# Identity products in TensorE's waits: linear attention and an FNet block with an MLP, on one Trainium2 core

## The chip, the cores and the metric

The kernel runs on 1 core of one Trainium2 chip. The metric is the device time of one execution in microseconds (us). Before the change the median of five runs is 843.5 us (841.67, 842.81, 843.5, 844.53 and 843.78). Where a stretch of one execution is described, the times are those of one further execution that was recorded with the hardware profiler.

## The reference

Four sequences (batches) of 768 rows with 8 heads of 64 columns go through causal linear attention with a decay `lam` per head. Its result `x` (768 rows of 512 columns for each batch) goes through a two-dimensional Fourier transform whose real part is added to it, a normalization of each row, and an MLP of 512 to 2048 to 512 with a ReLU. Everything is float32; the two weight matrices arrive as float64.

```
intra = einsum(q, k) * Dmask            # Dmask = lam ** (i - j), i >= j
out   = einsum(intra, v) + einsum(q * lam_pow, kv_state)
u     = x + real(fft(fft(x, axis=1), axis=2))
un    = (u - mean) / sqrt(var + 1e-6)
y     = u + relu(un @ w_ch1) @ w_ch2
```

## The kernel before, in words

**Attention** (`attn`, lines 241 to 387) cuts the 768 rows of a batch into six chunks of 128. For each chunk `attn_in` loads k, q and v (SP's queue), transposes k and q on TensorE by a product with the identity (L268, L273) and lets ScalarE copy the results out of PSUM (L270, L275); VectorE also writes the decayed copy `qs` (L279). `attn_out` multiplies k by q into scores (L292); VectorE multiplies each half of the scores by the decay (L296, tiles `sc`); TensorE updates the running state (L307, then L309 or L312 on VectorE), multiplies the old state by `qs` (L320) and the scores by v (L324). ScalarE copies the result `oT` out (L327), and `back` transposes it into rows (L340, then L342 and L343 on ScalarE). Batch 0 is "turned": the rows in mirrored order that the Fourier transform needs are made by TensorE too (`mirrored`, on tile `ds`); the other batches write their rows to DRAM and gather them mirrored (L421, L424, L429 on GpSimd's queue).

**The Fourier transform** (`fft_ln`) folds the rows by symmetry on VectorE (L410 to L413, L448 to L459), multiplies by cosine and sine tables along the rows (L483, copied out to `ys` by ScalarE at L487) and then along the columns (`width`, L496 to L501). ScalarE copies a part into `bs` (L559, L560, L562) and VectorE finishes `u` (L563 to L567).

**The normalization** (`norm`) takes statistics on VectorE (L513, L514), the root on GpSimd (L517, L518), and writes `un` on VectorE (L531; one buffer). For the first four pairs of tiles, the list `PLAIN`, TensorE transposes `un` (L536) and ScalarE copies it out to `ut` (L537), which the MLP reads. `PLAIN[0]` is the first pair of batch 0 whose rows are ready.

**The MLP** multiplies by the first weights (L600) and the second (L614) for `PLAIN`, and later, for all other rows, by a two-by-two scheme with seven products (L687, L734). The **weights** come in 32 pieces as float64 (L209, tile `raw`, four buffers shared with the MLP's hidden rows) and are turned into float32 by two ScalarE and five VectorE instructions each (L214, L216; L215, L218, L220, L221, L222). The pieces 0 to 7 fill the half of the first matrix that the first MLP half reads, 8 to 15 the half of the second matrix.

**The order of the work.** The program is written as generators that are woven together by planned durations (`weave`, `beside`, `run`): attention of batch 0 beside weight pieces; then attention of batch 1 beside the transform of batch 0 and more weight pieces; then the first half of the MLP beside what is left, and so on. On top of it a scheduler orders each engine's instructions by its own estimate of when their inputs are ready; the order in the built program is therefore not the order of the text. PSUM has five banks for the attention and the transform (`pa`) and three for the MLP (`pm`). An instruction wrapped in `keep_in_program_order` may not be placed ahead of the instruction that the text has before it on the same engine.

Of the kernel before, what the change touches and what calls it, by code (L numbers as in the profile page):

```python
# [76 lines left out]
def kernel(  # L77
# [10 lines left out]
    nc = tc.nc  # L88
# [50 lines left out]
    def new(pool, shape, tag, **kw):  # L139
        cnt[0] += 1  # L140
        return pool.tile(shape, F32, tag=tag, name=f"{tag}{cnt[0]}", **kw)

    def psum_a(shape):
        return new(pa, shape, "pa")

    def psum_m(shape):
        return new(pm, shape, "pm")

# [2 lines left out]
    ident = const.tile([128, 128], F32, name="ident")  # L154
# [128 lines left out]
    def attn_out(b, c, head):  # L283
        kT, qT, qs, kd, vt = ins.pop((b, c))
        last = c == NC - 1


        mm = nc.tensor.matmul
        pss = [psum_a([C, HP, C]) for _ in range(2)]
        for hp in range(HP):  # L290
            for hi in range(2):
                mm(pss[hi][:, hp, :], lhsT=kT[HD[hi], hp, :], rhs=qT[HD[hi], hp, :], start=True, stop=True)  # L292
        sc = []
        for hi in range(2):
            t = new(at, [C, HP, C], "sc", bufs=3)
            nc.vector.tensor_tensor(t, pss[hi], decay[:, hi::2, :], op=ALU.mult)  # L296
            sc.append(t)
        yield 1.5


        s_old, s_new = st[(c + 1) % 2], st[c % 2]
        if not last:
            pu = psum_a([128, HP, D])
            for hp in range(HP):
                for hi in range(2):
                    h = 2 * hp + hi
                    mm(pu[HD[hi], hp, :], lhsT=kd[:, h, :], rhs=vt[:, h, :], start=True, stop=True)  # L307
            if c == 0:
                nc.vector.tensor_copy(s_new, pu)  # L309
            else:  # L310
                nc.gpsimd.tensor_tensor(s_new, s_old, spow.broadcast_to([128, HP, D]), op=ALU.mult)
                nc.vector.tensor_tensor(s_new, s_new, pu, op=ALU.add)  # L312
            yield 0.9


        po = psum_a([128, HP, C])
        if c > 0:
            for hp in range(HP):
                for hi in range(2):
                    mm(po[HD[hi], hp, :], lhsT=s_old[HD[hi], hp, :], rhs=qs[HD[hi], hp, :],  # L320
                       start=(hp == 0), stop=False, skip_group_check=True)
        for hp in range(HP):
            for hi in range(2):
                mm(po[HD[hi], hp, :], lhsT=vt[:, 2 * hp + hi, :], rhs=sc[hi][:, hp, :],  # L324
                   start=(c == 0 and hp == 0), stop=(hp == HP - 1), skip_group_check=True)
        oT = new(at, [128, HP, C], "oT")
        nc.scalar.copy(oT, po)  # L327
        if b in TURNED:

            if c == 0:  # L330
                nc.scalar.copy(first, po[:, :, 0:1])
            elif c > 1:
                nc.scalar.copy(oTs[b][:, :, 0:1], po[:, :, 0:1])
        yield 2.0
        yield from head

        def back(oT, x, n=128):
            px = psum_a([C, HP, 128])
            for hp in range(HP):
                nc.tensor.transpose(px[:, hp, :], oT[:, hp, :], ident)  # L340
            px = px.rearrange("p h e -> p (h e)")
            nc.scalar.copy(x[0:n, 0:HM], px[0:n, 0:HM])  # L342
            nc.scalar.copy(x[0:n, HM:DM], px[0:n, DM - 1:HM - 1:-1])  # L343

        if b not in TURNED:
            x = xn_[b, c] = new(xp, [C, DM], "x") if c < HC else new(xn, [C, DM], "xn")
            back(oT, x)
            if c == 0:
                xd[b] = (dram.tile([S - 256, DM], F32, name=f"xa{b}"), dram.tile([257, DM], F32, name=f"xb{b}"))
                nc.scalar.dma_start(xd[b][1][256:257], x[0:1])  # L350
            elif not last:
                nc.scalar.dma_start(xd[b][0][(c - 1) * C:c * C], x)
            if c >= NC - 2:
                nc.scalar.dma_start(xd[b][1][(c - NC + 2) * C:(c - NC + 3) * C], x)
            if c == NC - 2:
                mirror_a(b)
            elif last:
                mirror_b(b)
            yield 1.7
            return  # L360


        if c == 2:
            eo[b] = new_eo()

        def mirrored(m):
            if m < HC:
                back(oTs[b], eo[b][HC - 1 - m][1][:, 1, 0:DM], BLK[HC - 1 - m])
            else:
                u = xs[b, HC + NC - 1 - m] = new(xp, [128, DM], "x")  # L370
                back(oTs[b], u)

        if c > 1:
            mirrored(c - 1)
            yield 1.4
        if c > 0:
            oTs[b] = new(fp, [128, DM + 4], "ds")[:, 0:DM].rearrange("p (h c) -> p h c", h=HP)
            nc.scalar.copy(oTs[b][:, :, C - 1:0:-1], po[:, :, 1:C])
        if not last:
            x = xn_[b, c] = new(xp, [C, DM], "x") if c < HC else new(xn, [C, DM], "xn")  # L380
            back(oT, x)
            yield 1.7
        else:
            nc.scalar.copy(oTs[b][:, :, 0:1], first)
            mirrored(c)
            for t in range(HC):
                xs[b, t] = xn_.pop((b, t))
            yield 1.4
# [26 lines left out]
    def mirror_a(b):  # L415

        xa = xd[b][0]

        eo[b] = new_eo()
        for a, n in enumerate(BLK):  # L420
            gather(out=eo[b][a][1][0:n, 1, 0:DM], out_offset=None, in_=xa[:, :], in_offset=row_of(a, n))  # L421
        for t in range(2, HC):
            u = xs[b, HC + t] = new(xp, [128, DM], "x")
            gather(out=u[:, :], out_offset=None, in_=xa[:, :], in_offset=row_of(2 + t))  # L424
# [45 lines left out]
    def fft_ln(b):  # L470
# [7 lines left out]
        for i in range(5):  # L478
            ps = psum_a([128, 2, NK])
            m = 128 if i < 4 else 1  # L480
            for n in range(2):
                for a, rows in enumerate(BLK):
                    mm = nc.tensor.matmul(ps[0:m, n, :], lhsT=piece(a, i, n), rhs=cs[0:rows, a, i in (2, 3), n, :],  # L483
                                          start=(a == 0), stop=(a == 1))
# [24 lines left out]
        def norm(g):  # L509
            mv = new(np_, [128, G, 2], "mv")  # L510
            for i in range(G):
                stt = new(np_, [128, 6], "stt")
                nc.vector.bn_stats(stt, xs[b, TT[g][i]])  # L513
                nc.vector.bn_aggr(mv[:, i, :], stt)  # L514
            ve = new(np_, [128, G], "ve")
            rs = new(np_, [128, G], "rs")
            nc.gpsimd.tensor_scalar(ve, mv[:, :, 1], EPS, None, op0=ALU.add)  # L517
            nc.gpsimd.tensor_tensor(rs, ve, mhalf, op=ALU.pow)  # L518

            yield 5.0 if (b, g) == PLAIN[0] else 1.0  # L520
            plain = (b, g) in PLAIN
            if plain:
                ut = uts[b, g] = new(up, [128, KO, G * 128], "ut")
            else:

                to = utd[b, g] = dram.tile([128, KO, G * 128], F32, name=f"utd{b}{g}")
            for i in range(G):
                un = new(np_, [128, DM], "un", bufs=1)
                u = xs[b, TT[g][i]]
                for o, x in ((un[:, 0:HM], u[:, 0:HM]), (un[:, HM:DM], u[:, DM - 1:HM - 1:-1])):  # L530
                    nc.vector.tensor_scalar(o, x, mv[:, i, 0:1], rs[:, i:i + 1],  # L531
                                            op0=ALU.subtract, op1=ALU.mult)
                if plain:
                    pt = psum_a([128, KO, 128])
                    for c in range(KO):
                        nc.tensor.transpose(pt[:, c, :], un[:, 128 * c:128 * c + 128], ident)  # L536
                    nc.scalar.copy(ut[:, :, 128 * i:128 * i + 128], pt)  # L537
                else:

                    uq = new(ep, [128, DM], "e")  # L540
                    nc.vector.transpose(uq, un)
                    for r in range(0, 128, 32):
                        dst = to[:, :, 128 * i + r:128 * i + r + 32].rearrange("(a d) c n -> d c a n", d=32)
                        src = uq[r:r + 32].rearrange("p (c a n) -> p c a n", c=KO, n=32)
                        nc.sync.dma_start(dst, src)
                yield 0.7
            if plain:
                return
            for T in TT[g]:
                ud[b, T] = dram.tile([128, DM], F32, name=f"ud{b}{T}")  # L550
                nc.sync.dma_start(ud[b, T], xs.pop((b, T)))

        for t in (1, 2, 0):
            ps = psum_a([128, DM])
# [14 lines left out]
            if t == 0:  # L569
                ps = psum_a([128, DM])  # L570
# [12 lines left out]
    PLAIN, LATE = ORDER[:4], ORDER[4:]  # L583
# [289 lines left out]
```

## Time and profile before

| what | value |
|---|---|
| median of five runs | 843.5 us |
| profiled execution, own time | 841.55 us |
| its span, first to last instruction | 839.5 us |
| around the span | 2.05 us |
| mean granted TensorE clock | 0.992 |
| PE busy | 801.8 us, 96%, 4608 instructions |
| VectorE (DVE) busy | 444.9 us, 53%, 1030 instructions |
| ScalarE (ACT) busy | 181.8 us, 22%, 436 instructions |
| GpSimd (POOL) busy | 77.7 us, 9%, 102 instructions |

PE is TensorE's products, PEld its weight loads. A float32 product that isn't a transpose stands in the trace as two instructions (x2 for one product), a transpose as one. In the page's second part each digit is the busy share of one of 40 equal slices of 21 us. The clock row is the TensorE clock that was granted, in tenths of full speed. "Idle before <- X" says how long an engine stood still ahead of an instruction and what released it.

### The profile page before, as it was taken

What the parts mean: (1) busy time and instruction counts of PE and PEld (TensorE: products, weight loads), DVE (VectorE), ACT (ScalarE), POOL (GpSimd) and SP (SyncE); (2) the same over time, 40 slices, a digit from 0 to 9 for tenths busy, and PEclk for the clock granted to TensorE, in tenths of its full rate; (3) what the DMA queues carried; (4) which work ended last, traced back from release to release, by engine and by line L of the source; (5) the groups of instructions that cost most, each with busy time, mean ns of one, the idle gap of its engine ahead of it and who ended that gap; (6) DMA issues with size and microseconds to landing.
All of it is one profiled execution on the core that took longest, in us unless ns stands there. A gap on an engine that the chain in (4) does not pass through costs nothing.

```text
span 839.5 us, 11685 instructions
## 1 busy us (share of the span) xinstructions
PE 801.8 (96%) x4608; PEld 639.3 (76%) x4608; DVE 444.9 (53%) x1030; ACT 181.8 (22%) x436; POOL 77.7 (9%) x102
## 2 busy tenths in 40 slices
PE   5977799999999999999999999999999999999998
PEld 4766576767766666767847888888888888888886
DVE  6969989875822483245795551155412552145411
ACT  3762542323511111221101210022000220012100
POOL 2211121010111020121000000000000000000000
PEclk9998899999999999999999999999999999999999
DMA  9967443138832136441334011100111000110010
GB/s 241 259 155 197 120 139 131 62 84 214 201 95 70 37 75 138 101 135 38 97 72 144 0 52 43 52 7 0 51 51 51 0 1 16 51 36 1 1 38 25
DMA packets 126683, 68.87 MB, mean 82 GB/s; under 512 B 111150, under 2 KB 112174, under 8 KB 126630
## 3 DMA queue, kind: packets, MB, share of 16 engines
q1 hardware_dynamic: 121632, 55.67, 26.0%
q0 software_dynamic: 2112, 6.69, 2.4%
q10 hardware_dynamic: 2886, 5.77, 1.9%
q8 instruction: 36, 0.59, 0.3%
q14 instruction: 17, 0.14, 0.1%
HBM read 48.72 MB, written 19.40 MB: 81 GB/s over the span
## 4 chain that ended last, share of the span: by engine, by line
PE 79%; DVE 11%; issue 4%; DMA 3%; ACT 2%; POOL 1%; SPq 0%; POOLq 0%; DVEq 0%; ACTq 0%
PE p L734 23%; PE p L687 23%; PE pm L614 9%; PE pm L600 7%; PE pa L324 3%; PE pa L292 3%; PE pa L483 3%; PE pa L320 2%; PE pa L340 1%; DMA x<-xb,ix 1%; PE pa L268 1%; PE pa L307 1%; DVE stt L513 1%; DVE sc L296 1%; DMA xb<-xn 1%
## 5 line engine op out<-in xcount | busy, mean ns | idle before, releaser
L600 PE MATMUL pm<-ut,w 128*128 128x256 f32 x512 | 119.8, 383 | 0.2 <-DVE hr L606 0.2
L614 PE MATMUL pm<-w,hr 128*128 128x512 f32 x256 | 116.1, 598 | 1.3 <-DVE hr L606 1.3
L600 PEld LDWEIGHTS pm<-ut,w 128*128 128x128 f32 x512 | 94.1, 190 | 15.6 <-issue 3.4
L687 PE MATMUL p<-ur,w 128*128 128x256 f32 x384 | 93.8, 379 | 0.0
L614 PEld LDWEIGHTS pm<-w,hr 128*128 128x128 f32 x256 | 46.6, 190 | 51.4 <-issue 48.6
L687 PEld LDWEIGHTS p<-ur,w 128*128 128x128 f32 x384 | 73.0, 190 | 10.3 <-issue 0.5
L687 PE MATMUL p<-us,w1s 128*128 128x256 f32 x256 | 65.7, 379 | 0.0
L734 PE MATMUL p<-w,hs 128*128 128x256 f32 x256 | 58.0, 379 | 0.5 <-DVE y L755 0.5
L734 PE MATMUL p<-w,ha 128*128 128x256 f32 x256 | 57.9, 379 | 0.0
L734 PE MATMUL p<-w2s,hs 128*128 128x256 f32 x256 | 57.9, 379 | 0.0
L734 PEld LDWEIGHTS p<-w,hs 128*128 128x128 f32 x256 | 48.5, 190 | 7.5 <-DVE y L755 0.9
L734 PEld LDWEIGHTS p<-w2s,hs 128*128 128x128 f32 x256 | 48.6, 190 | 6.6
L687 PEld LDWEIGHTS p<-us,w1s 128*128 128x128 f32 x256 | 48.6, 190 | 6.6
L734 PEld LDWEIGHTS p<-w,ha 128*128 128x128 f32 x256 | 48.6, 190 | 6.6
L589 POOL DMA_INDIRECT out_dram<-y,ix x12 | 11.8, 987 | 408.2 <-DVE y L760 344.1
L714 ACT COPY ha<-p 128x256 f32<-128x256 f32 x32 | 11.9, 372 | 169.2 <-PE p L687 139.4
L292 PEld LDWEIGHTS pa<-qT,kT 64*128 64x128 f32 x384 | 28.2, 198 | 17.1 <-ACT qT L275 9.7
L292 PE MATMUL pa<-qT,kT 64*128 64x128 f32 x384 | 33.2, 299 | 7.1 <-ACT qT L275 6.7
L296 DVE TENSOR_TENSOR sc<-pa,decay 128x512 f32<-128x512 f32 x48 | 31.6, 683 | 12.7 <-PE pa L292 12.5
L324 PE MATMUL pa<-sc,v 128*64 128x128 f32 x384 | 31.7, 287 | 6.1 <-DVE sc L296 6.1
L725 DVE TENSOR_TENSOR ha<-p,ha 128x256 f32<-128x256 f32 x32 | 13.6, 425 | 44.8 <-ACT ha L724 44.8
L324 PEld LDWEIGHTS pa<-sc,v 128*64 128x64 f32 x384 | 23.2, 140 | 14.8 <-DVE sc L296 9.1
(144 smaller groups left out, 1139.6 us busy)
## 6 DMA issues: line engine op xcount, KB each, us to landing
raw<-in_moe_w_ch_dram SPq DMA_DIRECT2D x32, 512.0 KB, 4.9
k<-in_k_dram SPq DMA_DIRECT2D x24, 256.0 KB, 4.7
q<-in_q_dram SPq DMA_DIRECT2D x24, 256.0 KB, 5.0
v<-in_v_dram SPq DMA_DIRECT2D x24, 256.0 KB, 3.3
ud<-x SPq DMA_DIRECT2D x16, 256.0 KB, 2.3
utd<-e SPq DMA_DIRECT2D x64, 64.0 KB, 2.2
u<-ud SPq DMA_DIRECT2D x16, 256.0 KB, 2.7
ur<-utd SPq DMA_DIRECT2D x6, 512.0 KB, 4.3
```

Source lines behind the costliest of these rows:

```text
L292: mm(pss[hi][:, hp, :], lhsT=kT[HD[hi], hp, :], rhs=qT[HD[hi], hp, :], start=True, stop=True)
L296: nc.vector.tensor_tensor(t, pss[hi], decay[:, hi::2, :], op=ALU.mult)
L320: mm(po[HD[hi], hp, :], lhsT=s_old[HD[hi], hp, :], rhs=qs[HD[hi], hp, :], start=(hp == 0), stop=False, skip_group_check=True)
L324: mm(po[HD[hi], hp, :], lhsT=vt[:, 2 * hp + hi, :], rhs=sc[hi][:, hp, :], start=(c == 0 and hp == 0), stop=(hp == HP - 1), skip_group_chec ...
L483: mm = nc.tensor.matmul(ps[0:m, n, :], lhsT=piece(a, i, n), rhs=cs[0:rows, a, i in (2, 3), n, :], start=(a == 0), stop=(a == 1))
L589: nc.gpsimd.indirect_dma_start(out=out.rearrange("b s d -> (b s) d"), out_offset=row_of(2 + HC * (b + 1) + T - HC), in_=y[:, :], in_offset ...
L600: nc.tensor.matmul(ps, lhsT=w1[:, c, 128 * fc:128 * fc + 128], rhs=ut[:, c, :], start=(c == 0), stop=(c == KO - 1))
L614: nc.tensor.matmul(ps, lhsT=hr[(fc - f0) // 4][:, fc % 4, 128 * i:128 * i + 128], rhs=w2[:, fc, :], start=(fc == f0), stop=(fc == f1 - 1))
L687: nc.tensor.matmul(ps, lhsT=s2.A[a][:, kt, 128 * i:128 * i + 128], rhs=U[b][:, kt, :], start=(first and kt == 0), stop=(kt == 1), skip_gro ...
L714: nc.scalar.copy(a11, two(X))
L725: V.tensor_tensor(a22, two(Z), a22, op=ADD)
L734: nc.tensor.matmul(ps, lhsT=h[a][:, s, i, :], rhs=s2.B[b][:, i, :], start=(first and i == 0), stop=(i == HF - 1), skip_group_check=True)
```

## The change

A helper `warm(n)` takes one PSUM tile of the MLP's pool and issues `n` products of the 128x128 identity with itself into it. Nothing reads the tile. It is called in four places: after the score products of chunks 0 to 2 of batch 1 (four products each), in the last chunk of batch 0 ahead of the first and the second of its two mirrored transposes (four and six), and ahead of the first normalized rows of `PLAIN[0]` (sixteen): 38 products in all. Each is kept behind the TensorE instruction that stands before it in the text. No other line changes.

```
+    def warm(n):
+
+        ps = psum_m([128, 128])
+        for _ in range(n):
+            tc.keep_in_program_order(nc.tensor.matmul(ps, lhsT=ident, rhs=ident, start=True, stop=True))
...
                 mm(pss[hi][:, hp, :], lhsT=kT[HD[hi], hp, :], rhs=qT[HD[hi], hp, :], start=True, stop=True)
+        if b == 1 and c < 3:
+            warm(4)
         sc = []
...
         if c > 1:
+            if last:
+                warm(4)
             mirrored(c - 1)
...
             nc.scalar.copy(oTs[b][:, :, 0:1], first)
+            warm(6)
             mirrored(c)
...
             for i in range(G):
+                if (b, g, i) == (*PLAIN[0], 0):
+                    warm(16)
                 un = new(np_, [128, DM], "un", bufs=1)
```

## The prediction, made before the changed kernel had run

> **What bounds the kernel now.** I read the page first: busy shares by slice, the granted clock and the chain that ended last.
>
> ```profile
> span 839.5 us, 11685 instructions
> PE   5977799999999999999999999999999999999998
> DVE  6969989875822483245795551155412552145411
> PEclk9998899999999999999999999999999999999999
> PE 79%; DVE 11%; issue 4%; DMA 3%; ACT 2%; POOL 1%; SPq 0%; POOLq 0%; DVEq 0%; ACTq 0%
> ```
>
> From the sixth slice on (105 us) PE is the bound and nearly full. Before that it waits, VectorE is at 9 in slices 4 to 6, and two slices have a lower clock. What is won or lost before about 116 us shifts everything behind it by as much. So I read that stretch in steps of 4 us (PE, PEld, DVE, ACT and POOL busy with counts, clock, DMA).
>
> ```profile
> core 0: us, PE busy (x) PEld busy (x) DVE busy (x) ACT busy (x) POOL busy (x), PEclk, DMA share, GB/s
> 64.00:68.00 4.00, 1.70 (x10) 0.85 (x8) 4.00 (x8) 1.17 (x2) 0.46 (x1) 1.00 0.85 298
> 68.00:72.00 4.00, 3.12 (x24) 2.39 (x26) 3.89 (x9) 1.25 (x4) 0.94 (x1) 0.62 0.30 67
> 72.00:76.00 4.00, 4.00 (x46) 3.49 (x42) 2.66 (x5) 1.18 (x3) 1.11 (x1) 0.53 1.17 304
> 96.00:100.00 4.00, 1.16 (x16) 0.97 (x16) 4.00 (x8) 1.39 (x4) 0.00 (x0) 0.96 0.76 188
> 100.00:104.00 4.00, 2.05 (x20) 1.62 (x20) 3.42 (x11) 1.41 (x3) 0.95 (x2) 0.50 0.01 2
> 104.00:108.00 4.00, 4.00 (x41) 3.27 (x38) 3.93 (x8) 1.08 (x3) 1.51 (x1) 0.69 0.02 4
> ```
>
> Twice a 4 us step with little PE work (1.70, 1.16 busy) is followed by some 7 us at half clock, and VectorE is full on both occasions: PE is waiting for VectorE. The timelines of PE and of VectorE show the instructions.
>
> ```profile
> 50.49 0.66 PE L340 MATMUL pa<-ident,ds 128*128 128x128 f32 x4 [0.74 <-ACT ds L333]
> 52.46 0.66 PE L340 MATMUL pa<-ident,ds 128*128 128x128 f32 x4 [1.32 <-ACT ds L384]
> 57.78 0.43 PE L324 MATMUL pa<-sc,v 128*64 128x128 f32 x2 [1.17 <-DVE sc L296]
> 77.56 1.09 PE L324 MATMUL pa<-sc,v 128*64 128x128 f32 x14 [1.12 <-DVE sc L296]
> 93.34 0.39 PE L499 MATMUL pa<-dt,ys 128*128 128x128 f32 x2
> 93.57 0.39 PE L501 MATMUL pa<-dt,ys 128*128 128x128 f32 x2
> 101.95 1.12 PE L536 MATMUL pa<-ident,un 128*128 128x128 f32 x4 [4.56 <-DVE un L531]
> 105.10 1.74 PE L320 MATMUL pa<-qs,st 64*64 64x128 f32 x16
> ```
>
> ```profile
> 61.05 0.69 DVE L279 TENSOR_TENSOR qs<-pa,qpow 128x512 f32<-128x512 f32 x1 [1.31 <-ACT qT L275]
> 73.34 0.69 DVE L296 TENSOR_TENSOR sc<-pa,decay 128x512 f32<-128x512 f32 x1 [1.46 <-PE pa L292]
> 90.71 0.42 DVE L312 TENSOR_TENSOR st<-st,pa 128x256 f32<-128x256 f32 x1 [0.34 <-PE pa L307]
> 95.24 0.42 DVE L563 TENSOR_TENSOR ds<-pa,bs 128x256 f32<-128x256 f32 x1
> 101.48 0.74 DVE L531 TENSOR_SCALAR un<-x,mv,rs 128x256 f32<-128x256 f32 x2 [0.58 <-POOL rs L518]
> ```
>
> The reader is to see the chain: VectorE from L279 (61.05) to L563 (95.24) with only two waits for PE (1.46 and 0.34), on to `un` (101.48), then PE through L536 to L501 at half clock, and the first MLP products (L600) at 109.89.
>
> **Part 1, the products themselves.** A 128x128 float32 product that isn't a transpose costs 0.22 us at full clock (L499 to L501, 93.34 to 93.57) and, as L320 takes 1.74 at half clock and 1.09 at full, about 0.44 at half. 38 x 0.22 = 8.4 us of PE work. Ahead of the two mirrored transposes: 4 x 0.22 = 0.88 in a wait of 0.74, 6 x 0.22 = 1.32 in one of 1.32: up to 0.15 later. Chunks 0 to 2 of batch 1: 0.88 each, ahead of L307, and PE waits 1.17, 1.84 (0.66 and 1.18) and 1.12 for `sc` soon after: nothing. Had VectorE been quicker it would be 0.88 each. L307's readers (the state on VectorE, `kd` on POOL, which waits for L307) follow 0.9 later and have 0.7 or more (L307 would end at 57.5, L309 starts at 58.23). Sixteen: 3.5 us in the wait of 4.56 ahead of L536: nothing at full clock, 7.0 at half. The `pm` banks aren't used by the MLP yet. Sum: +0.15.
>
> **Part 2, the clock.** From L536 (101.95) to L496 (107.80) before: 5.85 us. At full clock, by start-to-start rows elsewhere: L536 0.51 (117.14 to 117.65), L307 0.62 (62.16 to 62.78), L536 0.51, L320 1.02 (62.78 to 63.80), L324 1.03 (106.77 to 107.80): 3.69. If the sixteen products keep the clock, PE gains 2.16, less about 0.3, because `un` has one buffer, so that its second half waits for the first L536 (a row at 116.58 waits 0.60 so). I take -1.85; bounds 0 (clock low all the same) and -2.16. The first stretch (70 to 76 us) is worth only what VectorE waited, 1.46 + 0.34, which goes into part 3.
>
> **Part 3, what moves.** The built program differs on every engine from batch 1's first chunk to 105 us; behind it the order is the same. On VectorE the score products of chunk 1 come up to 2 us earlier in the fold, the second one of chunk 2 comes later, behind the fold of the second block, and above all the conversions of weight pieces 14 and 15, which stood behind `un`, now stand ahead of L563. One conversion takes 2.2 us there, by the starts from 84.01 on: L215 0.33, L220 0.34, L218 0.33, L221 0.60, L222 0.60. L563 before: 34.19 after L279, 32.39 of it without the two waits. Added: 4.4 for pieces 14 and 15, 0.6 for piece 13's L222, which stood behind L564. Taken off: 0.6 for piece 9's L221, which moves ahead of L279 into the 1.31 that VectorE waits there. 36.8: L563 at 97.85 instead of 95.24, if no new wait arises. From L563 to `un` 6.24, now 5.64 without the L222: `un` at 103.5, +2.0. Behind `un` VectorE is free of 4.4 us of work, but the next norm waits for PE, so nothing is gained there. Bounds for this part: 0, if VectorE's moved work falls into time that the chain waits for others anyway, and +4.4, if the waits of 1.8 come back elsewhere and a collision or two is added (L412 at 63.46 and L455 at 74.62 take 1.28 beside POOL's L264, for 0.41 alone).
>
> PE in between: `sc` for the second half of chunk 2 ends at about 79.8 (before 77.43), so PE stands nearly 7 us ahead of L324, with one product in it; the four added ones lie ahead of L307, not in this wait. A half clock is then likely at 76 to 86. From L324 to the end of chunk 3's L292: 1.0 + 1.4 (four L483) + 0.9 (L268, L273) + 1.4 + 0.6 (L340) + 1.4 + 1.1 = 7.8 at full clock: 87.6. With two steps of 3.4 us at half, 91.0. VectorE comes to that chunk's `sc` with 6.5 us to go to L563, at 91.3: just covered.
>
> Here the Trainium skill, "TensorE: Matmul & The Clock Gate", section "Part 1: The HAM clock gate", speaks for the sixteen and against the fours: the clock is judged over free-running windows of 3413 ns and falls to half after an idle one. The trace's rows agree as far as they go. By that rule 0.88 us can't fill a window, and the half clock only moves from 69 to about 76; the sum stays as above, since it is covered. The same page, section "Part 4: PE-mode transpose", says that transposes don't count as PE-busy in the same way; were that decisive, the low clock would last longer and VectorE would wait too, perhaps 1 us more.
>
> Other queues. SP: piece 14's load goes ahead of chunk 5's k and q, piece 15's behind them and still ahead of v; loads of a piece land 3.7 us after issue there (89.52, 86.36). The buffer of piece 11 is free at about 85, the load lands by 92 at the latest, and L215 wants it at 93. ACT: its two steps per piece (0.6 each) go between the copies of `ys`; the last of these stands behind piece 15's first step. POOL: same order. Nothing, with about 1 us of cover.
>
> **Sum.** +0.15 - 1.85 + 2.0 = +0.3 us on the profiled execution: 841.55 to 841.85. That execution is 1.95 below the median. The runs spread by 2.9 us, the size of the two half-clock stretches (2.2 and 1.8), so I take it that they differ by where the clock falls; with the second stretch gone the changed kernel should stay nearer to the quick one. Between 841.85 and 843.8 (0.3 on the median) I take the middle, 842.8.
>
> **The rivals.**
> *Forecast, 0.39:* clock won, VectorE's order lost, about even; its own range is 841.8 to 845.2.
> *A, faster, 0.32:* the moved conversions cost less than 2.0, as VectorE's new order meets waits of its own or loses collisions; with 0.3 - 2.0 from the profiled execution 839.9, from the median 841.8; I name 841.0. For it: VectorE waits 1.8 less for PE. Against: VectorE at 4.00 of 4 in most steps.
> *B, slower, 0.17:* the clock is already half when the sixteen start (about 98.8). They then take 7.0 and end at 105.8 instead of 102.3; `un` is there at 103.5. It decides from 4.7 us on, a clock under 0.75. L536 then comes 1.8 us later than in the forecast (104.0), and if the clock returns only behind it, the 1.85 is lost as well: +2.1 to +3.9, 845.0 to 846.6. Against: PE is full from 80 to 96.
> *C, the change doesn't do what it says, 0.12:* half clock at the same places, or longer at 80 to 90, so that VectorE waits for chunk 3's scores or for `ys` behind piece 15's load: 0.3 + 1.85 on the median, 845.7.
>
> **Numbers.** A measurement of this kernel tells about 0.2% (1.7 us) from no change. Faster is A and a sliver of the forecast, 0.33; slower is B and C, 0.29; same 0.38. The range, 839.9 to 846.6, is from A's lower end to B's upper.
>
> **What would show it.** Clock 1.00 from 96 to 108 us and L536, L307, L536, L320 in 2.7 us instead of 4.8; sixteen products ahead of L536 in 3.5; `un` at 103 to 104; first L600 at 110 to 110.5; low clock once, between 75 and 86. Wrong, if `un` comes before 102 or after 105, or if the sixteen run at half clock.

## The result, and the profile after

The changed kernel takes 846.5 us (median of 38 runs, 843.08 to 849.81), the kernel before beside it 843.32 us (median of 64 runs, 839.78 to 847.73). The ratio is 1.0036, 95% interval 1.0028 to 1.0044: slower by some 3 us, beyond the 0.2% that counts as no change. The profiled execution of the changed kernel has a time of its own of 847.47 us and a span of 845.6. Single executions differ by more than that (6.7 us from the fastest to the slowest here), so a profile shows where time goes in one execution, and only medians say what a change is worth.

The page of the changed kernel first (lines of the changed kernel are 6 to 13 higher than those of before: L296 is L304, L324 is L332, L483 is L494, L531 is L544, L536 is L549, L563 is L576, L600 is L613, L614 is L627).

```profile
span 845.6 us, 11838 instructions
PE   5996998999999999999999999999999999999998
DVE  5969968884933574236696561145411552145411
PEclk9998999999999999999999999999999999999999
PE 74%; DVE 5%; issue 3%; DMA 2%; POOL 1%; ACT 0%; POOLq 0%; DVEq 0%; ACTq 0%
```

The third and the fifth slice of PE are now full, the fourth (63 to 85 us) has a gap, and one slice instead of two shows a lower clock; it is the one with the gap. By steps of 4 us (the columns as in the prediction: PE, PEld, DVE, ACT and POOL busy with counts, clock, DMA share, GB/s):

```profile
72.00:76.00 4.00, 1.74 (x34) 1.43 (x33) 4.00 (x10) 0.86 (x2) 1.20 (x1) 1.00 1.05 285
76.00:80.00 4.00, 0.38 (x2) 0.14 (x2) 4.00 (x11) 0.20 (x1) 0.00 (x0) 0.65 0.64 254
80.00:84.00 4.00, 2.88 (x17) 2.56 (x18) 4.00 (x12) 1.57 (x3) 1.79 (x1) 0.50 0.00 0
84.00:88.00 4.00, 4.00 (x19) 3.91 (x18) 3.15 (x8) 2.47 (x5) 3.63 (x1) 0.57 0.72 202
100.00:104.00 4.00, 3.73 (x39) 3.61 (x40) 3.97 (x9) 0.77 (x3) 0.00 (x0) 1.00 0.83 197
104.00:108.00 4.00, 3.16 (x35) 2.34 (x34) 2.79 (x8) 0.59 (x1) 1.45 (x3) 1.00 0.02 6
```

The second stretch went as meant: the clock is 1.00 from 96 to 108 us, where before it fell to 0.50 and 0.69. The first one came back in another place, 77 to 87 us. The timeline of PE shows what it cost, and a third place that the prediction didn't look at.

```profile
75.95 0.43 PE L332 MATMUL pa<-sc,v 128*64 128x128 f32 x2 [2.27 <-DVE sc L304]
81.11 1.97 PE L332 MATMUL pa<-sc,v 128*64 128x128 f32 x14 [4.73 <-DVE sc L304]
101.36 3.84 PE L153 MATMUL pm<-ident 128*128 128x128 f32 x32
106.04 0.76 PE L549 MATMUL pa<-ident,un 128*128 128x128 f32 x4 [0.84 <-DVE un L544]
110.48 0.49 PE L507 MATMUL pa<-dt,ys 128*128 128x128 f32 x2
112.57 0.60 PE L613 MATMUL pm<-ut,w 128*128 128x256 f32 x2
144.32 0.89 PE L494 MATMUL pa<-cs,fe 128*128 128x193 f32 x4 [2.68 <-DVE fe L463]
145.05 3.23 PE L627 MATMUL pm<-w,hr 128*128 128x512 f32 x4
```

From L549 to L507 4.44 us instead of 5.85. But the first MLP product comes at 112.57 instead of 109.89, 2.7 late; about 0.9 of that is there at 40 us already, where nothing but the place in time differs. And the wait ahead of L494 at 144 us is 2.68, and the four products L627 behind it run at half clock. Before, the same rows were

```profile
139.69 0.89 PE L483 MATMUL pa<-cs,fe 128*128 128x193 f32 x4 [0.85 <-DVE fe L452]
140.42 1.88 PE L614 MATMUL pm<-w,hr 128*128 128x512 f32 x4
```

At the second L494 (148.07 against 142.13) PE is 5.9 late, soon 6.2, and stays so to the end. So in these two profiles some 1.8 us come from the stretch of the change and 3.3 from 136 to 148 us, where both kernels have the same order of instructions on every engine.

The timeline of VectorE, for the same stretch:

```profile
62.16 0.69 DVE L285 TENSOR_TENSOR qs<-pa,qpow 128x512 f32<-128x512 f32 x1 [0.46 <-ACT qT L281]
88.25 0.69 DVE L285 TENSOR_TENSOR qs<-pa,qpow 128x512 f32<-128x512 f32 x1 [1.10 <-ACT qT L281]
92.03 1.28 DVE L304 TENSOR_TENSOR sc<-pa,decay 128x512 f32<-128x512 f32 x2
99.79 0.42 DVE L576 TENSOR_TENSOR ds<-pa,bs 128x256 f32<-128x256 f32 x1
105.57 0.73 DVE L544 TENSOR_SCALAR un<-x,mv,rs 128x256 f32<-128x256 f32 x2 [0.58 <-POOL rs L529]
140.85 0.69 DVE L421 TENSOR_TENSOR fe<-x,x 128x512 f32<-128x512 f32 x1 [2.61 <-DMA x<-xb,ix]
```

From the query product L285 of chunk 1 to `un` VectorE needs 43.41 us (before: 61.05 to 101.48, 40.43). There is a new wait of 1.10 for PE's late transposes (through ScalarE's copy). And at 140.85 VectorE waits 2.61 for the gathered rows; before it was

```profile
136.22 0.69 DVE L410 TENSOR_TENSOR fe<-x,x 128x512 f32<-128x512 f32 x1 [0.78 <-DMA x<-xb,ix]
```

What is late there is the store of the last chunk to DRAM (`xb<-xn`) and, with it, the gather that reads it back mirrored (`x<-xb,ix`). Below I call this the late gather. The transfers from the store's issue to the gather's issue (queue: packets, MB, share of 16 engines; then the issue with its time to landing), before:

```profile
q10 hardware_dynamic: 144, 0.26, 29.9%
q1 hardware_dynamic: 12, 0.03, 3.6%
xb<-xn ACTq DMA_DIRECT2D x1, 256.0 KB, 2.0
```

and in the changed kernel:

```profile
q10 hardware_dynamic: 144, 0.26, 23.9%
q1 hardware_dynamic: 13, 0.04, 3.4%
q8 instruction: 1, 0.02, 2.2%
xb<-xn ACTq DMA_DIRECT2D x1, 256.0 KB, 2.8
```

There is one packet more, of the queue q8 that the page calls "instruction". It is 16 KB, starts 0.19 us behind the store's issue and holds one of the DMA engines for 1.05 us; the store's last packet ends 2.27 us behind its issue instead of 1.67. The gather's own issue on POOL then takes 2.31 us instead of 1.45 (before, then after):

```profile
132.42 1.45 POOL L429 DMA_INDIRECT x<-xb,ix  x1 [4.76 <-DMA xb<-xn]
135.96 2.31 POOL L440 DMA_INDIRECT x<-xb,ix  x1 [5.49 <-DMA xb<-xn]
```

### The profile page after: what moved, and what is told of

Its sections match the earlier page's. It is cut to its first block, busy times and chain, and to the rows that moved or that the text cites. A ratio compares the mean times of both kernels' runs of the same rounds, so it can differ in the third digit from the quotient of the medians.

```text
span 845.6 us, 11838 instructions
## 1 busy us (share of the span) xinstructions
PE 810.1 (96%) x4684; PEld 647.7 (77%) x4684; DVE 444.4 (53%) x1030; ACT 182.3 (22%) x436; POOL 82.7 (10%) x102
## 4 chain that ended last, share of the span: by engine, by line
PE 74%; DVE 5%; issue 3%; DMA 2%; POOL 1%; ACT 0%; POOLq 0%; DVEq 0%; ACTq 0%
PE p L747 23%; PE p L700 23%; PE pm L627 10%; PE pm L613 8%; PE pa L494 2%; PE pa L332 2%; PE pa L298 2%; DMA x<-xb,ix 1%; PE pa L328 1%; DMA xb<-xn 1%; PE pa L348 1%; PE pa L274 1%; PE pa L315 1%; PE pa L279 1%; DVE un L544 1%
## 5 line engine op out<-in xcount | busy, mean ns | idle before, releaser
L613 PE MATMUL pm<-ut,w 128*128 128x256 f32 x512 | 119.8, 383 | 0.2 <-DVE hr L619 0.2
L627 PE MATMUL pm<-w,hr 128*128 128x512 f32 x256 | 117.4, 604 | 1.3 <-DVE hr L619 1.3
L613 PEld LDWEIGHTS pm<-ut,w 128*128 128x128 f32 x512 | 94.1, 190 | 15.6 <-issue 3.4
L627 PEld LDWEIGHTS pm<-w,hr 128*128 128x128 f32 x256 | 46.9, 191 | 51.7 <-issue 48.9
L332 PE MATMUL pa<-sc,v 128*64 128x128 f32 x384 | 32.4, 292 | 9.5 <-DVE sc L304 9.5
L298 PEld LDWEIGHTS pa<-qT,kT 64*128 64x128 f32 x384 | 26.4, 193 | 16.6 <-ACT qT L281 10.3
L298 PE MATMUL pa<-qT,kT 64*128 64x128 f32 x384 | 31.2, 293 | 7.0 <-ACT qT L281 7.0
L332 PEld LDWEIGHTS pa<-sc,v 128*64 128x64 f32 x384 | 23.9, 143 | 18.2 <-DVE sc L304 12.6
L304 DVE TENSOR_TENSOR sc<-pa,decay 128x512 f32<-128x512 f32 x48 | 31.5, 683 | 11.2 <-PE pa L298 11.0
L738 DVE TENSOR_TENSOR ha<-p,ha 128x256 f32<-128x256 f32 x32 | 13.6, 425 | 44.9 <-ACT ha L737 44.9
```

Source lines behind the costliest of these rows:

```text
L613: nc.tensor.matmul(ps, lhsT=w1[:, c, 128 * fc:128 * fc + 128], rhs=ut[:, c, :], start=(c == 0), stop=(c == KO - 1))
L627: nc.tensor.matmul(ps, lhsT=hr[(fc - f0) // 4][:, fc % 4, 128 * i:128 * i + 128], rhs=w2[:, fc, :], start=(fc == f0), stop=(fc == f1 - 1))
L738: V.tensor_tensor(a22, two(Z), a22, op=ADD)
```

## The experiments

Three theories came out of the two traces. *Order*: the moved instructions cost, above all on VectorE. *Products*: the products themselves cost, whatever the order. *Later gather*: the loss at 136 to 148 us has a cause of its own. No line but the products' was changed, so the moved order is the scheduler's answer to them. Where a kernel gets "the order of" another, the same instructions are traced, and neighbours in a table are tied together in issue order without a wait:

```python
for table in ORDER_OF.values():          # by engine: instruction numbers in the order wanted
    chained = [named[f"I-{n}"] for n in table if f"I-{n}" in named]
    for x, y in zip(chained, chained[1:]):
        tc.add_manual_dep(y, x.name, DependencyInfo(NoSync, DATA), reason="hold_order")
```

All times are medians; the kernel before measured 842.87 to 843.43 beside them. Products of the identity are never read, so none of these kernels computes anything else than the kernel before. "Lateness" is the start of a PE instruction less that of the same one in the profile of before; a negative one is early. "Half clock" is a granted clock of 0.50.

### Order and products apart

All 38 products with the order of before on VectorE, ScalarE, SP and PE (the diff against the changed kernel is the table):

```diff
+    ORDER_OF = {"DVE": ..., "Activation": ..., "SP": ..., "PE": ...}   # as the kernel before issues
+    hold_order()
```

> All 38 products stay; VectorE, ScalarE, SP and PE (the products aside) issue in exactly the order of the kernel before. Order theory (the loss comes from the moved VectorE work, chiefly the conversions of weight pieces 14 and 15 ahead of L563 of before): un comes at 101 to 102 again, the clock stays at 1.00 from 96 to 108 us, and the time is about 1.7 us under before, 841.6 (840.8 to 842.5). Rival, the products themselves cost (PE work in front of L307 of before and of the mirrored transposes): as slow as the changed kernel, 846 to 847. Rival, the later wait for the gathered rows at 136 to 145 us costs whatever stands in the early order: 844 to 846 with 2 us or more of PE idle ahead of L483 of before.

And the reverse, the kernel before with the order of the changed one and no product:

```diff
+    ORDER_OF = {"DVE": ..., "Activation": ..., "SP": ..., "PE": ...}   # as the changed kernel issues
+    hold_order()
```

> The kernel before with no product added, but VectorE, ScalarE, SP and PE issue in exactly the order of the changed kernel. Order theory: un at 104 to 105.5, the half clock at 100 to 107 us comes back since nothing fills the wait ahead of L536 of before, so even slower than the changed kernel by the 1.85 us of the clock: about 848 (846.5 to 849). Rival, the products cost: 843.3, as before. Rival, later gather wait: 844 to 846.

Measured beside the changed kernel itself:

> The changed kernel once more, beside the other three. All theories: 846.5 in the median. Order theory: most of the loss stands at 112 us already (1.8 to 2.7 against before) and PE's wait at 136 to 145 us differs from one profile to the next. Rival, later gather wait: again 2 us or more of PE idle ahead of L494 (L483 of before) and a half clock right behind it.

Products in the old order: 841.13, ratio 0.9978 [0.9965, 0.9991]. New order without products: 848.58, 1.0062 [1.0039, 1.0085]; without one of its six executions, which took 4043 us, the median is 848.10. The changed kernel again: 845.43, 1.0025 [1.0012, 1.0039]. So the order costs 4.3 us with the products (845.43 less 841.13) and 4.9 without (848.10 less 843.22); the products bring 2.1 in the old order and 2.7 in the new one. The order theory holds, the theory of the products falls. What I had not expected is where the products bring it: in the old order `un` comes 38.03 us behind L285 of chunk 1 instead of 40.43; the half clock at 69 to 76 us, and with it VectorE's wait for the scores, is gone. The page and the steps of that kernel:

```profile
span 840.4 us, 11836 instructions
PEclk9999999999999999999999999999999999999999
```

```profile
64.00:68.00 4.00, 3.20 (x44) 2.32 (x42) 4.00 (x8) 0.59 (x1) 1.06 (x1) 1.00 1.10 315
68.00:72.00 4.00, 2.63 (x30) 2.03 (x31) 4.00 (x10) 1.69 (x4) 0.94 (x1) 1.00 0.18 46
72.00:76.00 4.00, 3.65 (x54) 2.92 (x51) 4.00 (x12) 1.35 (x4) 1.62 (x1) 1.00 1.14 293
```

The clock there was 1.00, 0.62 and 0.53 before. One expectation missed: the PE wait at the gather was 2 us and more here as well (VectorE 2.44, lateness from -2.4 at 136 us to +0.9 at 144), while the kernel without products had none of it (0.9 on VectorE, +6.4 and +6.5). So the late gather goes with the products, not with the order.

### Sixteen alone

> Of the products the sixteen ahead of the first L536 of before alone; all engines issue in the order of the kernel before. Order theory: the clock is held from 96 to 108 us and nothing else changes, 841.5 (840.8 to 842.5). Rival, the products cost: the sixteen end before un comes, so at most 0.3 over before, 843.3 to 843.6, and no gain. Rival, later gather wait: L497 to L563 earlier makes the gather no earlier, so what is won is given back as PE idle at 136 to 140 us, 843.

```diff
-        if b == 1 and c < 3:
-            warm(4)
...
-            if last:
-                warm(4)
...
-            warm(6)
...
+    ORDER_OF = {...}   # as the kernel before issues
```

845.15, 1.0024 [1.0007, 1.0042]: slower than before, against all three theories. Its profiled execution took 848.69, 3.5 over its median, so it shows a bad case. In it the sixteen bring 0.7 (lateness 4.0 at 96 us, 3.3 at 108), not the 1.85 expected; `un` comes soon behind them. 1.1 are lost at 52 to 56 us to a half clock that no profile with the ten products of batch 0's end shows, 2.2 more from 64 to 80 (half clock at 70 and again at 80, the fours are missing), and 3.3 at the gather. There the instruction packet (1.6 us, at 121.81) falls behind the store to `xa` at 120.96, the gather L424 of before behind that takes 1.73 to issue instead of 0.98, and its packets are still on their way when the next store is issued.

### The late gather and PE's instruction packets

The page of before has 36 packets of q8 for 9216 records of PE (4608 product instructions and as many weight loads): 256 records a packet, and as one float32 product makes two of each, 64 such products. So I take q8 for the fetches of PE's own instructions; the trace doesn't name their engine. The Trainium skill, "Runtime: NRT & Kernel Launch", section "Instruction fetch mechanics", says that engines refill instruction memory in blocks of 16 KiB, 256 instructions, through a DMA queue of their own, which agrees with these counts, and that crossing a block's border is mostly hidden, which was to be tested. If the packets are PE's, 38 products more must bring each packet earlier by 0.6 of a block, and 64 put them back. Small products (64x16) at the start of the program, where PE waits for the first loads, move the packets and nothing else of the stretch:

```diff
+    def pad(n):
+        ps = psum_m([128, 128])
+        for _ in range(n):
+            tc.keep_in_program_order(nc.tensor.matmul(ps[0:64, 0:16], lhsT=ident[:, 0:64], rhs=ident[:, 0:16],
+                                                      start=True, stop=True))
...
+        if (b, c) == (0, 0):
+            pad(13)
         pss = [psum_a([C, HP, C]) for _ in range(2)]
...
+    pad(13)
     att1, mix = attn(1), fft_ln(0)
```

> All 38 products, every engine in the order of the kernel before, and 26 more small products of the identity (64x16) in the idle time of PE at the start: 13 ahead of the first L268 of before, 13 ahead of the first L292. 38 + 26 = 64 products are 256 PE instructions of 64 bytes, as many as one instruction packet of 16 KB holds, so that PE's fetches should fall where they fell in the kernel before. Fetch theory (the extra PE instructions move a fetch to just behind the store xb<-xn at 128 to 133 us, which lands later and with it the gather x<-xb,ix): no fetch between that store's issue and the gather, the store lands in 2.0 instead of 2.8 us, the gather's issue takes 1.45 instead of 2.2, VectorE waits 0.8 instead of 2.4 for it, and the time is 839.4 (838.3 to 840.3). Rival, the store and the gather are slow for another reason that comes with the products: 841.1, as without the 26.

> The kernel before, its order on all engines unchanged, with 38 small products of the identity at the start only (19 ahead of the first L268, 19 ahead of the first L292), none in the stretch of the change. Fetch theory: PE's instruction packets come as early as in the changed kernel, one of them within 0.5 us behind the store xb<-xn at 130 us; VectorE waits 2.4 instead of 0.8 for the gathered rows and PE comes 1.6 (no half clock there) to 3.3 us (half clock) later behind 140 us: 844.9 to 846.6. Rival, the products have nothing to do with that wait: 843.3, as before.

> The changed kernel, in its own order, with the 26 small products at the start that fill up one instruction packet. Fetch theory: the wait for the gathered rows is back to 0.8 us on VectorE and the loss at 136 to 148 us goes; what is left is the moved order less the clock, so 1.6 to 3.3 under the changed kernel: 843.5 (842.5 to 844.5). Rival, another reason: 845.4 to 846.5, as the changed kernel.

> The kernel before, in its order, with 64 small products at the start (32 and 32), a whole instruction packet more. Fetch theory: the fetches behind 60 us fall as in the kernel before, so 843.3 (842.3 to 844.3), while 38 cost 1.6 or more. Rival, early products cost or bring something by themselves (the clock at the start, a later first L268): the same sign and about 1.7 times as much as with 38.

| kernel | us | ratio to before |
|---|---|---|
| old order, 38 products, 26 early | 838.79 | 0.9942 [0.9921, 0.9962] |
| before, 38 early | 844.69 | 1.0019 [1.0006, 1.0032] |
| changed, 26 early | 843.30 | 0.9996 [0.9977, 1.0015] |
| before, 64 early | 847.89 | 1.0055 [1.0033, 1.0077] |

The kernel before with 38 early products has the late gather without a product in the changed stretch. Its transfers from the store to the gather:

```profile
q10 hardware_dynamic: 144, 0.26, 22.3%
q1 hardware_dynamic: 13, 0.04, 3.2%
q8 instruction: 1, 0.02, 2.2%
xb<-xn ACTq DMA_DIRECT2D x1, 256.0 KB, 2.8
```

VectorE waits 2.57 there, and PE's lateness goes from 0.6 at 136 us to 4.0 at 144. With 26 more the changed kernel has none of it:

```profile
139.25 0.69 DVE L429 TENSOR_TENSOR fe<-x,x 128x512 f32<-128x512 f32 x1 [0.80 <-DMA x<-xb,ix]
```

and its lateness is 3.0 from 104 us to the end. 841.13 to 838.79 and 845.43 to 843.30: 2.3 and 2.1 us for moving the packets, 1.5 in the kernel before (844.69 less 843.20); each of these differences of medians is uncertain by a microsecond or more, and the rows of the profiles carry the argument. "Mostly hidden" doesn't hold where a packet falls right behind a transfer that others wait for. The 64 were a miss in the time, not in the mechanism: 32 products at half clock held the first L268 up from 4.95 to 8.67 us, and lateness is 5.9 from 20 us on; at the gather it stays at 5.9, no packet lies behind the store, and VectorE doesn't wait longer. In all seven profiles with 38 products the packet lies 0.2 to 0.7 us behind the store's issue, and the lateness grows there by 1.6 to 3.6; in the six with none or 64 (38 and 26, or 64 early) it doesn't lie there, and the lateness grows by 0.1 at most.

The size goes with the clock. Behind the late gather the records show a half clock of 3.41 us in five of the seven (3.0 to 3.6 lost) and none in two (1.6 and 2.0). Why the gather's issue takes 2.1 to 2.4 us in six of the seven was not tried. In the six profiles with none or 64 it takes 1.1 to 1.5; with the sixteen alone it takes 2.3 without a packet behind this store.

### Which part of the order

Relative to before, VectorE's order differs chiefly in the scores of chunk 2 (the second behind the second block's fold) and in the conversions (those of pieces 11 to 13 earlier, those of 14 and 15 ahead of L576 and not behind `un`). Each put back alone in the changed kernel, as lines of VectorE's order:

```diff
 L464 TensorTensor fe       # scores_back
 L467 TensorTensor fo
-L304 TensorTensor sc       (chunk 2, first)
+L304 TensorTensor sc       (chunk 2, second; the first goes ahead of L459)
 L469 TensorTensor fo
...
 L544 TensorScalarPtr un    # conversions_back
+L221 L226 L221 ... L228    (pieces 14 and 15, from ahead of L576)
```

> The changed kernel in its own order on all engines, except that VectorE's two score products of batch 1's chunk 2 (L304) stand where the kernel before has them: the second ahead of the first block's last fold steps (L469) and not behind the second block's. Theory that the late scores cost (PE idles 5 us ahead of L332 and runs at half clock from 75 to 87, so that VectorE meets a wait at L285): the half clock there goes, un comes 1 to 2 us earlier, 844.4 (843.5 to 845.2). Theory that the conversions of pieces 14 and 15 ahead of L576 cost (4.4 us of VectorE): VectorE stays full from L285 to L576, so 845.4 to 846.5 as the changed kernel.

> The changed kernel in its own order on all engines, except that the conversions of weight pieces 14 and 15 (VectorE and the ScalarE steps that go with them) stand behind un again, as in the kernel before. Theory of the conversions: L576 and un come 3 to 4.4 us earlier relative to L285 at 62 us, 842.6 (841.8 to 843.6); the late gather at 136 to 145 us stays. Theory of the late scores: PE's half clock at 75 to 87 us makes VectorE wait for the scores of chunk 3 in place of the conversions, so at most 1 us is won, 844.6 to 845.5.

848.09, 1.0054 [1.0033, 1.0074], and 845.99, 1.0037 [1.0023, 1.0052], against 845.43 for the changed kernel: neither brought anything, and each theory by itself fell. With the conversions back VectorE has 4.4 us less to do and waits instead:

```profile
92.45 0.42 DVE L320 TENSOR_TENSOR st<-st,pa 128x256 f32<-128x256 f32 x1 [1.17 <-PE pa L315]
96.32 0.43 DVE L576 TENSOR_TENSOR ds<-pa,bs 128x256 f32<-128x256 f32 x1 [3.44 <-ACT ds L575]
```

PE, late by the scores, sets the end. With the scores back PE is earlier, VectorE has no wait from 80 us to L576 and comes no sooner, since the conversions are there. `un` comes late for PE then,

```profile
102.88 1.08 PE L549 MATMUL pa<-ident,un 128*128 128x128 f32 x4 [2.54 <-DVE un L544]
```

the sixteen end at 100.3, and a half clock follows from 102.5 to 112.8: L549 to L507 took 7.72 us. So the third theory: two limits side by side, of which each hides the other.

> The changed kernel in its own order, with both at once: the scores of chunk 2 and the conversions of pieces 14 and 15 where the kernel before has them. Theory of two limits side by side (PE, late by the scores, and VectorE, full with conversions, reach L576 at about the same time, so that either alone hides the other): VectorE's L285 of chunk 1 to un takes 40.4 us or less instead of 42.2 to 43.4, and the time is 843.5 (842.5 to 844.5), the late gather's 2 us included. Rival, what costs is a third part of the order (the conversions of pieces 11 to 13 ahead of chunk 3's L285, PE's L494 kept together ahead of chunk 3's L298): un stays where it is in either alone, 845 to 847.

> The same with the 26 small products at the start, which put PE's instruction packets back to where the kernel before has them. Two limits: 841.3 (840.3 to 842.3), 2.2 under the run without them. Rival, third part: 843 to 844.5, about as the changed kernel with the 26 (843.3).

Both at once: 842.98, 1.0000 [0.9989, 1.0012], and with the 26 early products 841.85, 0.9983 [0.9971, 0.9995]. From L285 to `un` 40.18 and 41.10 us, against 43.41 and 42.24 in the changed kernel, 42.33 with the scores alone and 41.73 with the conversions alone. VectorE, now relieved, still waits for PE ahead of L576:

```profile
95.98 0.43 DVE L576 TENSOR_TENSOR ds<-pa,bs 128x256 f32<-128x256 f32 x1 [3.17 <-ACT ds L575]
```

Two limits it is, for 2.5 us (845.43 less 842.98), or 1.5 with the 26 (843.30 less 841.85); the 26 bring 1.1 here instead of the 2.2 expected. The other 2 to 3 us to the 38.0 of the old order stay with the rest of the moved order (a half clock from 77 us on is still there in both profiles); which part of it was not tried.

### What the products are worth in the old order

> The sixteen products in the order of the kernel before (845.15 without more), with 8 small products at the start, so that 24 products stand ahead of 105 us: by the rates of the fetches (a packet per 64 products, 16 us apart at 105 to 122 us, 25 at 122 to 147) the packets should come about 6 us ahead of the store xa<-x at 121 us and between the two gathers from xb, not behind a store. Fetch theory: VectorE waits 0.8 for the gather again and the time falls by 2 to 3 us, 842.6 (841.6 to 843.6), although fewer products than 64 are added. Rival, only a whole packet's worth puts things right or the sixteen cost by themselves: 845.

> The products ahead of the mirrored transposes (4 and 6) and of L315 (3 x 4) without the sixteen, in the order of the kernel before, with 2 small ones at the start (24 in all, the same place of the fetches as with the sixteen and 8). If the fours hold the clock at 70 to 76 us and PE's lateness there counts: about 2.3 under before with the half clock at 100 to 107 still there, 841 (840.3 to 842). If, as the prediction had it, that stretch is worth only what VectorE waited and the sixteen bring 1.85: 842.5 to 843.3, slower than with the sixteen and 8.

The edits are `pad(4)` and `pad(4)` on the kernel with the sixteen, and `pad(1)` and `pad(1)` on one without them. 844.12, 1.0017 [1.0003, 1.0031], and 841.63, 0.9983 [0.9969, 0.9997]. So it is the fours and the ten that bring the time, and the sixteen little: lateness from 60 to 76 us falls by 3.4 with the fours (0.1 to -3.3) and by 0.2 without (1.9 to 1.7), and the sixteen bring 0.7 (1.7 to 1.0). My place for the packets was wrong: with 24 products they lie at 119.84 and 114.89, right behind the stores to `xa` at 118.70 and 114.21, not 6 us ahead. The gather from `xa` took 1.73 instead of 0.98, which cost 0.5 and 0.4; the wait at the last gather was gone all the same.

> The quickest version once more (all products, the order of the kernel before, 26 small products at the start), measured beside the two others: 838.8 (838 to 839.6), with the clock at 1.00 from 15 us to the end. If the gain were an accident of that series it would be nearer to 841.

838.85, 0.9954 [0.9938, 0.9971] (838.78 without one of its six executions, which took 1197 us): the version with all 38 products, the order of before and the packets in their old place is quicker than both kernels, and it holds. In both of its profiles the clock stays full once it has become so; the first one's page:

```profile
span 835.0 us, 11937 instructions
PEclk9999999999999999999999999999999999999999
```

## Why the prediction was wrong

It said 842.8, and "same" as likeliest; measured were 846.5, slower. The largest miss comes first.

- **The step that failed: "behind it the order is the same", so nothing.** Behind 105 us the prediction put the change at nothing. The runs showed 2.1 to 2.3 us there (1.6 to 3.6 in the profiles), at 136 to 148 us: 38 products more move PE's instruction packets, and one of 16 KB comes to lie right behind the store that the gather waits for. With 26 products more, which move it away, the changed kernel takes 843.30 against 843.20 of the kernel before. So for the stretch ahead of 112 us the sum of +0.3 holds as far as the medians tell (+0.1; the interval is -1.9 to +1.3). The profiles show +1.8 there in the one and +0.6 in the other of the changed kernel.
- **That the sum came so near is in part luck.** Taken apart, the moved order costs 4.3 to 4.9 us, not 2.0, and the products, with their packets out of the way, bring 4.4, not 1.7. The two misses cancel.
- **Part 1, +0.15.** Right as far as the mirrored transposes go: with the order of before lateness goes from 0.7 to 0.8 there. That the other products would be hidden was right for PE's time. It was wrong that they cost nothing elsewhere: as instructions they move PE's fetches.
- **Part 2, -1.85.** The mechanism held, the clock stood at 1.00 from 96 to 108. 5.85 us became 4.44, so -1.4 in this count; against the same order without the products (7.22) it is -2.8. In the order of before the sixteen are worth 0.7. The term depends on when `un` comes, and the prediction took it for a constant. The sixteen took 3.84 us, against 3.5 forecast.
- **Part 3, +2.0 (0 to +4.4).** L285 to `un` took 3.0 more, and 1.8 more in the second profile of the changed kernel; the forecast lies between. (`un` came at 105.57, past the 105 that was named as a sign of being wrong; 0.9 of that is the late start.) VectorE's own work was forecast well: from L285 to L576 37.63, or 36.53 without a wait of 1.10, and 36.47 in the second profile, against 36.8. The reason given was half of it. "Added: 4.4 for pieces 14 and 15" is no cost by itself, as undoing it alone brought nothing: PE, late by the scores and at half clock, is a second limit, about equal to the first. "Just covered" was reckoned at chunk 3's `sc`, and there it held: VectorE comes to it at 92.03 without a wait. It failed a step earlier, at chunk 3's L285, which needs PE's transposes of q and which the prediction didn't look at. There VectorE waits 1.10 where the clock stays low for 10.24 us, and not at all where it stays low for the two windows of 3.4 that I reckoned with (6.83 in the second profile).
- **The clock rule beside part 3.** I concluded that 0.88 us "can't fill a window" and that the half clock only moves. In the new order it did move, to where I put it (75 to 86; 77 to 87 in the profile), and PE stood the "nearly 7 us" ahead of L324 (2.27 and 4.73). In the order of before the fours removed it. The Trainium skill, "TensorE: Matmul & The Clock Gate", section "Part 1: The HAM clock gate", speaks of an idle window. In the 17 profiles here (PE's busy share between 20 and 800 us in steps of 3.41 us, laid out from one of the clock's changes) the steps need not be idle: at full clock every step with a share of 0.39 or less was followed by half clock, of those from 0.41 to 0.53 eight of thirteen were, and none with 0.54 or more was. A few products can lift a step over that: in the order of before the lowest step between 60 and 76 us has 0.36 to 0.53 without the fours and 0.60 or more with them.
- **The middle, 842.8.** I took it that runs differ by where the clock falls in the two stretches, and that the changed kernel would stay nearer to the quick one. Its runs spread over 6.7 us. One thing in which executions differ is when the clock first becomes full, 13.6 to 19.3 us in profiles whose starts are the same program, and PE's lateness at 20 us follows it (-1.6 at 13.6, +0.9 at 19.1). That is 2.5 of the 5.5 us between the two profiles of the changed kernel. The sum on the median, 843.8, would have been nearer, and 2.7 short.
- **The rivals.** The measured time lies in the range that rival B was given, but B didn't happen: the sixteen ran at full clock. (Nor does that range follow from its terms: +2.1 to +3.9 is 845.6 to 847.4 on the median and 843.65 to 845.45 on the profiled execution.) The loss of the clock happened in another kernel and by another way: in scores_back the sixteen ended too early, and the clock fell behind them. Of C its second half, VectorE waiting for a late PE, is what the changed kernel's first profile shows, at L285. A's premise, that part 3 costs clearly less than 2.0, isn't what the profiles show (3.0 and 1.8).
- **A reading.** VectorE is at 9, 9 and 8 in slices 4 to 6 of the page before, not at 9 in all three; nothing rests on it.

Median against median, the account is: order +4.3, products -4.4 with their packets out of the way, packets +2.3, together +2.2 in the series of these runs (845.43 against 843.22). The first series, with 38 executions, has 3.2; where the 1.0 between them lies isn't shown. Of the order's 4.3 the two limits explain 1.5 to 2.5; the rest stays open.

## What to carry to other kernels

Compare the order of the built programs before the durations: 38 tiny products, hidden in PE's waits, let the scheduler choose another order that cost 4 us, and tying the old order turned a loss of 2 to 3 us into a gain of 2. Two engines that arrive together hide each other: undo both parts before a cause is called innocent. Where instructions are added to a long program, look at the instruction packets too; if one comes to lie behind a transfer that others wait for, some padding in an idle place moves it away, as long as the place is idle: 26 small products cost nothing there, 64 cost 4.7 us.

## What the runs showed of the hardware

- An instruction packet of 16 KB holds one DMA engine for 0.9 to 1.6 us. Right behind the issue of a store of 256 KB it came with that store landing in 2.7 to 2.9 us, 3.5 in one profile, where 2.0 to 2.4 was seen in the profiles with none or 64 products added. Where the packets lie isn't proportional to the products added: 16 and 24 put a packet at the same place relative to PE's other work (about 118.5 us on the clock of before, with 121.9 without any), 38 at 110.2.
- Granted half-clock stretches of 3.41, 6.83, 10.24 and 13.65 us were seen, all multiples of 3.41; a wait of about 2.5 us on PE at the late gather cost 3.0 to 3.6 us where the step around it had a PE share of 0.25 to 0.37 (half clock followed, five profiles) and 1.6 and 2.0 where it had 0.46 and 0.42 (none followed).
